# Sliding-window attention and spatial-shift MLP on one core: z tiles taken 13 products behind a block's transfer, the first four token tiles of QKV in two parts, Y's rows returned two blocks later, W1's casts moved

## The chip, the core and the metric

The kernel runs on one core of a Trainium2 chip. The metric is the device time of one execution in microseconds (us). Five engines run their own instruction streams in order: PE (TensorE), DVE (VectorE), ACT (ScalarE), POOL (GpSimd) and SP (SyncE, which here issues almost all DMAs). They meet only through semaphores, so an instruction that waits holds back all that stands behind it on its engine.

## What is computed

```python
x = A_x                                   # [1, 2048, 576], f32
xn = _layernorm(x)
return x + A(xn, wqkv, wo) + B(xn, w1, w2, w3, w4)
# A: qkv = xn @ wqkv, 32 heads of 18; each token attends to the 8 tokens
#    0, 2, ... 14 behind it; times wo
# B: z = _layernorm(xn); h = gelu(z @ w1); four quarters of h shifted by +1, -1, +2, -2 tokens;
#    x1 = xn + h_shifted @ w2; x1 + gelu(_layernorm(x1) @ w3) @ w4
```

## The kernel before

Tokens are 16 tiles of 128; `Y[:, t, :]` holds tile t's 576 columns. Products are made in pairs of rounded parts: a cast on ACT gives the high part, a subtraction on DVE the low part, and PE adds three of the four partial products. Three stages matter here.

**QKV, plain part (0 to 86 us).** `wqkv` is cut in six column groups `cg` of 288. `units` lists 36 pairs (t, cg), each 14 matmuls (`q_part`, L396) into a PSUM tile `p1`, then a copy to a staging tile and a spill to DRAM (`q_leave`, L401 and L384). The first tiles are written out by hand ahead of the loop. A token tile gets there by `stats_x` and `norm_x` (DVE, with a power on POOL between them, L113), `tails` (a POOL copy of 64 columns, widened, L295), `turn_x`/`turn_main` and `turn_tail` (PE transposes into the PSUM tile `ps`, L303 and L307), and `cast_main`/`cast_tail` (ACT high part, DVE low part). Then the dictionaries `mids` and `plan` say which side work follows which unit. A tensor's tile counts as one thing: what writes into a PSUM tile waits for the earlier reads of the same tile.

**QKV, Strassen part (86 to 216 us).** Tiles 6 to 15 are done in blocks p = 3..7 of two tiles, each three column groups `g` of seven products of seven matmuls (`step`, `seven`, L581). A block has 21 slots, one for each product; `plan[slot]` lists side work that is issued after it. During block p the operands of the next block, n = p + 1, are made: `prep_lower` (slot 3) and `prep_upper` (slot 7), both through the one PSUM tile `pp`, then casts. ACT's `act.copy(raw[:, 2, :], ...)` (L357) and DVE's L358 write to rows of Y that `away` has spilled to DRAM (`ysp`, L547) to make room. Beside this each block makes z for four token tiles, twice-normalized x: `z_turn` scales on ACT and transposes on DVE into the one tile `ST` (L129, L130), and `put` sends `ST` to DRAM (`xd`, L137, four DMAs). A z tile of the next block can be written to `ST` only when these DMAs have read it. In block 7 `get` fetches z's first 512 tokens back and `split_x` casts them; `split_w1` casts W1, which lies in Y's first five rows.

**Mixing (216 to 284 us).** For four blocks b of 512 tokens, `mix_tile` makes four tiles of h (L715) and `mix_rem` (L730) the rest with W1R, whose parts travel by `v<-u` DMAs. z of block b + 2 is fetched at the end of block b, and its casts stand on ACT between two gelus (L720, L721). `back` (L572) reads the eight spilled rows of Y again.

SP issues all these DMAs in program order. In all of it the order is that of the code.

Of the kernel before, what the change touches and what calls it, by code (L numbers as in the profile page):

```python
# [57 lines left out]
def fused_block(ctx, tc, x, wqkv, wo, w1, w2, w3, w4, out):  # L58
# [85 lines left out]

    def split_x(xt, part=None, scr=None):
        raw = xt.bitcast(F32)
        if part != 1:
            r = xt[:, 9, :] if scr is None else scr.bitcast(F32R)
            act.copy(r[64:128], raw[64:128, 4, :])
# [3 lines left out]
        for h in range(2) if part is None else (part,):  # L153
# [55 lines left out]
    def load_x(t):  # L209
        sp.dma_start(Y[:, t, :], xf[t * 128:(t + 1) * 128, :])  # L210

    counted, scaled = set(), {}

    def stats_x(t):
        stats(Y[:, t, :], 0, t)
        counted.add(t)

    def norm_x(t):
        norm(Y[:, t, :], Y[:, t, :], 0, t)
        lo = t - t % 2  # L220
        if not scaled.get(lo) and counted >= {lo, lo + 1}:
            scaled[lo] = True
            two = slice(lo, lo + 2)
# [4 lines left out]
            for k in (lo, lo + 1):  # L228
                pool.tensor_tensor(RS[1][:, k, 1:2], RS[1][:, k, 0:1], mhalf, op=ALU.pow)

    qraw = {}
# [18 lines left out]
    def flat(v):  # L250
        return v.rearrange("p o s c -> p o (s c)")
# [102 lines left out]
    def prep_lower(p, ps):  # L354
        turned(2 * p + 1, ps)
        raw = raw_s(p)
        act.copy(raw[:, 2, :], ps[:, 0, 0:384])  # L357
        dve.tensor_tensor(raw[:, 0, :], ps[:, 1, 0:384], raw[:, 2, :], op=ALU.add)  # L358
        cast_a(x_ops(("p", p)), 2, 1, ps[:, 1:2, :])

    def prep_upper(p, ps):
        turned(2 * p, ps)
# [72 lines left out]
    for i in range(24):  # L435
# [25 lines left out]
    cast_x(1, True)  # L461
    q_part(pq[1], 1, 0, 0, 12)
    norm_x(2)
    tails(2)
    q_part(pq[0], 0, 0, 12, 14)
    q_leave(pq[0], 0, 0)
    q_part(pq[1], 1, 0, 12, 14)
    stats_x(3)
    turn_x(2)
    turn_tail(2, turns[2])  # L470
    q_leave(pq[1], 1, 0)
    norm_x(3)
# [20 lines left out]
    mids = {2: lambda: prep_x(3), 19: lambda: prep_x(4),  # L493
            20: lambda: prep_x(5), 28: lambda: lower(3), 30: lambda: upper(3)}
    plan = {
            2: ((split_cg, 3),),
            3: ((load_x, 5), (lambda: load_cg(2, raw_tile("rawc")),)),
            4: ((sums_b, 0, 0),), 5: ((sums_b, 0, 1),),
            6: ((split_cg, 1),), 7: ((split_t, 0, False),),
            8: ((lambda: load_cg(5, raw_tile("rawb")),),),  # L500
# [4 lines left out]
            20: ((sums_b, 2, 0), (load_x, 9)), 21: ((sums_b, 2, 1),), 22: ((stats_x, 7),),  # L505
            23: ((norm_x, 7), (tails, 7)), 24: ((stats_x, 6),), 25: ((norm_x, 6), (tails, 6)),
            26: ((split_t, 0, True),), 27: ((split_t, 2, False),),
            28: ((split_t, 1, True), (load_x, 11)),
            30: ((lambda: cast_upper(3, two[3]),), (load_x, 10)), 31: ((cast_s, 3, 0),),
            32: ((cast_s, 3, 1), (stats_x, 9)), 33: ((cast_s, 3, 2),), 34: ((split_t, 2, True),),  # L510
            35: ((norm_x, 9), (stats_x, 8))}
    for n, (t, cg) in list(enumerate(units))[2:]:
        q_plain(t, cg, mids.get(n))
        for f, *args in plan.get(n, ()):
            f(*args)
# [124 lines left out]
    for p in range(3, 8):  # L640
        n = p + 1
        if n < 8:
            q4 = 4 * (p - 3)
            zs = (q4 + 1, q4 + 2, q4 + 3, q4) if p == 4 else range(q4, q4 + 4)
            plan = {k: ((z_turn, t),) for k, t in zip((1, 9, 10, 17), zs)}
            plan.update({0: ((norm_x, 2 * n),), 3: ((low2, n),), 4: ((tails, 2 * n),),
                         7: ((up2, n),), 8: ((lambda n=n: cast_upper(n, two[n]),),),
                         14: ((cast_s, n, 0),), 15: ((cast_s, n, 1), (cast_s, n, 2))})
            plan[17] += ((put, ("z", p - 3)),)
            if n < 7:  # L650
                plan[4] += ((stats_x, 2 * n + 3),)
                plan[16] = ((stats_x, 2 * n + 2),)
                plan[17] += ((norm_x, 2 * n + 3), (tails, 2 * n + 3))
            plan[18] = {3: ((load_x, 13), (load_x, 12), (away, 0, 3)),
                        4: ((load_x, 15), (load_x, 14), (away, 3, 5))}.get(p, ())
            if p == 4:
                plan[11] = ((away, 5, 8),)
            if p == 5:
                plan[11] = ((load_w1,),)
# [1062 lines left out]
```

## Time and profile before

| | us |
|---|---|
| three runs: median (lowest, highest) | 1310.93 (1308.13, 1311.07) |
| the profiled execution: its time | 1308.89 |
| its span from first to last instruction | 1307.1 |
| mean granted TensorE clock | 0.987 |

The page gives each engine's busy share of the span; the waits give, for each engine, who ended its idle time; a timeline gives single instructions with the idle time ahead of each in square brackets and what released them. Matmuls overlap their weight loads, so PE is near full where its share is 97 to 99%.

### The profile page before, as it was taken

The numbers are of one execution on the slowest core, as the hardware profiler recorded it, in microseconds if no ns is written. First come the engines' busy times: TensorE is split into PE (matmuls) and PEld (weight loads), VectorE is DVE, ScalarE is ACT, GpSimd is POOL, SyncE is SP. The second block draws the span as 40 slices with busy tenths as digits, with TensorE's granted clock in tenths as the row PEclk, the third lists the DMA queues.
The fourth block names the chain that finished last, engine by engine and source line by source line (L and its number), as shares of the span: only waits on it lengthen the run. The fifth ranks groups of instructions, "written<-read, shape, count | busy, mean of one in ns | idle before, by whom it ended". The sixth has DMA issues, their size and how long they took to land.

```text
span 1307.1 us, 21009 instructions
## 1 busy us (share of the span) xinstructions
PE 1268.6 (97%) x7819; PEld 1166.0 (89%) x7819; DVE 933.2 (71%) x1206; ACT 766.1 (59%) x1276; POOL 264.3 (20%) x407
## 2 busy tenths in 40 slices
PE   8997888999999999999999999999999999999999
PEld 7997887789889999999879999999989989889898
DVE  7875544476847898999657898898999884455342
ACT  4453445443654554554677767777667777677730
POOL 3121100002132212111212322222123223222100
PEclk9998889899999999999999999999999999999999
DMA  8535767525688879587948898887967878899982
GB/s 228 142 78 145 195 143 195 157 70 174 183 189 215 200 184 183 118 193 168 203 100 197 179 204 198 185 174 180 271 126 156 165 135 155 190 219 217 252 255 82
DMA packets 208654, 228.92 MB, mean 175 GB/s; under 512 B 80920, under 2 KB 142328, under 8 KB 208424
## 3 DMA queue, kind: packets, MB, share of 16 engines
q1 hardware_dynamic: 175800, 160.79, 43.0%
q0 software_dynamic: 32752, 66.80, 31.8%
q8 instruction: 61, 1.00, 0.3%
q14 instruction: 41, 0.34, 0.1%
HBM read 127.71 MB, written 110.23 MB: 182 GB/s over the span
## 4 chain that ended last, share of the span: by engine, by line
PE 63%; issue 3%; ACT 2%; DVE 2%; DMA 1%; POOL 0%; DVEq 0%; POOLq 0%; ACTq 0%
PE ps L1120 30%; PE cc L1382 19%; PE p L1084 10%; PE ps L183 4%; DMA yd<-Y 1%; DVE xt L849 0%; DVE w3st L1217 0%; POOL yd L1126 0%; ACT Y L1125 0%; PE p L1689 0%; ACT xt L1179 0%; ACT Y L1067 0%; DVE c L1078 0%; DVE Y L1131 0%; ACT c L1072 0%
## 5 line engine op out<-in xcount | busy, mean ns | idle before, releaser
L1120 PEld LDWEIGHTS ps<-w,c 128*128 128x128 f32 x3456 | 478.8, 189 | 21.1 <-ACT Y L1125 2.0
L1120 PE MATMUL ps<-w,c 128*128 128x288 f32 x3456 | 489.9, 297 | 5.1 <-DVE c L1078 1.4
L1126 POOL DMA_DIRECT2D yd<-Y x154 | 138.1, 900 | 395.8 <-ACT Y L1125 336.3
L1078 DVE TENSOR_TENSOR c<-Y,c 128x512 fp32r<-128x512 f32 x144 | 98.9, 687 | 93.2 <-ACT Y L1067 91.7
L1125 ACT COPY Y<-ps 128x576 f32<-128x576 f32 x154 | 97.9, 637 | 76.1 <-PE ps L1120 66.1
L1382 PE MATMUL cc<-xt,w3s 128*128 128x512 f32 (+1 forms) x504 | 127.9, 393 | 0.9 <-DVE Y L1392 0.9
L1382 PEld LDWEIGHTS cc<-xt,w3s 128*128 128x128 f32 (+1 forms) x504 | 92.2, 188 | 19.3 <-DVE Y L1392 1.3
L1128 ACT COPY Y<-ps 128x576 f32<-128x576 f32 x92 | 58.9, 640 | 66.2 <-PE ps L1120 64.5
L1382 PE MATMUL cc<-x1n,w3a 128*128 128x512 f32 (+1 forms) x336 | 86.4, 396 | 0.0
L998 DVE TENSOR_TENSOR po<-q,k 128x1152 f32<-128x1152 f32 (+1 forms) x48 | 84.2, 1755 | 0.8
L1001 DVE TENSOR_REDUCE L<-po 128x64 f32<-128x1152 f32 (+1 forms) x48 | 84.0, 1751 | 0.8
L1066 ACT ACTIVATE c<-p 128x512 fp32r<-128x512 f32 x48 | 28.7, 597 | 85.5 <-PE p L1084 85.5
L1392 DVE TENSOR_TENSOR Y<-cc,Y 128x512 f32<-128x512 f32 x49 | 33.7, 688 | 59.4 <-ACT Y L1388 55.2
L974 DVE TENSOR_TENSOR po<-v,L 128x1152 f32<-128x1152 f32 x56 | 75.4, 1354 | 0.9
L396 PE MATMUL p<-wb,xt 128*128 128x288 f32 (+1 forms) x504 | 71.2, 299 | 2.1 <-ACT stg L401 0.8
L396 PEld LDWEIGHTS p<-wb,xt 128*128 128x128 f32 (+1 forms) x504 | 67.7, 189 | 4.1 <-ACT stg L401 1.0
L1382 PEld LDWEIGHTS cc<-x1n,w3a 128*128 128x128 f32 (+1 forms) x336 | 61.3, 190 | 11.3 <-DVE w3a L1228 0.5
L113 POOL TENSOR_TENSOR rs<-rs,mhalf 128x1 f32<-128x1 f32 x32 | 19.5, 609 | 237.0 <-DVE rs L112 118.6
L978 DVE TENSOR_TENSOR po<-po 128x1152 f32<-128x1152 f32 x49 | 66.4, 1355 | 0.9
L581 PE MATMUL ca<-wb,xt 128*128 128x288 f32 x420 | 65.0, 307 | 1.8 <-DVE keep L592 1.3
L581 PEld LDWEIGHTS ca<-wb,xt 128*128 128x128 f32 x420 | 61.2, 200 | 2.7 <-DVE keep L592 1.8
L1101 ACT COPY ps<-Y 128x576 f32<-128x576 f32 x92 | 59.4, 646 | 4.4 <-DVE Y L1131 2.4
(255 smaller groups left out, 2158.2 us busy)
## 6 DMA issues: line engine op xcount, KB each, us to landing
yd<-Y POOLq DMA_DIRECT2D x156, 288.0 KB, 6.2
Y<-in_B_w_dram SPq DMA_DIRECT2D x29, 576.0 KB, 5.9
w3st<-in_B_w_dram SPq DMA_DIRECT2D x56, 256.0 KB, 8.1
qkvd<-stg SPq DMA_DIRECT2D x66, 144.0 KB, 3.0
yd<-ev POOLq DMA_DIRECT2D x26, 288.0 KB, 6.4
w3st<-in_B_w_dram SPq DMA_DIRECT2D x92, 64.0 KB, 8.0
xd<-st SPq DMA_DIRECT2D x16, 320.0 KB, 4.9
xd<-big SPq DMA_DIRECT2D x16, 320.0 KB, 6.4
```

Of the source, the lines that this page charges most:

```text
L396: pe.matmul(ps[:, :QB], xo[:n, o + k, a, :], W[:n, w + k, v, :], start=i == 0, stop=i == len(PLAIN) - 1)
L581: pe.matmul(ps[:, :QB], xo[:n, XO[x], a, :], W[:n, OP[w], v, :], start=start and i == 0, stop=stop and i == len(HALVES) - 1, skip_group_ch ...
L974: dve.tensor_tensor(dst, vv, Lf[:, :, w:w + 1].to_broadcast([128, TPP * GH, HD]), op=ALU.mult)
L978: dve.tensor_tensor(o, o, dst, op=ALU.add)
L998: dve.tensor_tensor(dst, qf[:, None, :].to_broadcast([128, n, TPP * GC]), win, op=ALU.mult)
L1001: dve.tensor_reduce(Lw[:, w:w + n, :], dst.rearrange("p w (x d) -> p w x d", d=HD), axis=AX.X, op=ALU.add)
L1078: dve.tensor_tensor(h[:, 1, :], g, h[:, 0, :].bitcast(F32), op=ALU.subtract)
L1084: pe.matmul(ps, W3[f][:, w, :], x1n[b][:, a, :], start=n == 0, stop=n == len(PAIRS) - 1)
L1120: pe.matmul(ps[:, k, :HF], h[:, col], w[:, p, k * HF:(k + 1) * HF], start=n == 0 and not seed, stop=n == len(seq) - 1, skip_group_check=True)
L1125: act.copy(e.rearrange("p (h c) -> p h c", h=2), ps[:, :, :HF])
L1126: pool.dma_start(yd[t], e, accum_op=ALU.add)
L1382: pe.matmul(ps, WX[w][:k, v, SLOT[w], :], area[sb][xk][:k, a, :], start=onto is None and i == 0, stop=last and i == len(HALVES) - 1, skip_ ...
```

## The change

- `split_x` takes parts: 0 (tail and first half, as before), 2 (tail alone), 3 (first half alone), 1 (second half).
- The powers for z (`scales`) are no longer issued in `norm_x` but at slots of the plans; the first weight group's tail is subtracted on POOL and not on DVE.
- The first four token tiles: tiles 2 and 3 too are done in two parts, with their casts ahead of the tail transposes; some loads change places.
- `prep_lower` casts first and adds then. In blocks 3 to 6 z tiles stand at slots 9, 10, 16, 17 (before: 1, 9, 10, 17), the two `stats_x` at slots 2 and 4 (before: 4 and 16).
- Block 7: z's fetch at slot 3 (before: 6), another order in its first group, z's casts at slots 12, 15 and 18, W1's first part at 14, the second and third behind the block, the last two in mixing after tiles 0 and 1.
- `back` is called at (b, i) = (2, 0) and not at (0, 3).

```diff
     def norm_x(t):
         norm(Y[:, t, :], Y[:, t, :], 0, t)
...
@@ prep_lower
         act.copy(raw[:, 2, :], ps[:, 0, 0:384])
+        cast_a(x_ops(("p", p)), 2, 1, ps[:, 1:2, :])
         dve.tensor_tensor(raw[:, 0, :], ps[:, 1, 0:384], raw[:, 2, :], op=ALU.add)
-        cast_a(x_ops(("p", p)), 2, 1, ps[:, 1:2, :])
@@ first tiles
-    split_tail(r0, 0, 0)
+    split_tail(r0, 0, 0, pool)
     cast_x(0, True)
+    cast_x(1, True)
+    q_head(1)
+    load_cg(1, raw_rows(10))
     stats_x(2)
...
     norm_x(2)
     tails(2)
...
+    q_tail(0)
+    turn_x(2)
     stats_x(3)
-    turn_x(2)
+    q_tail(1)
+    cast_x(2)
     turn_tail(2, turns[2])
-    q_leave(pq[1], 1, 0)
     norm_x(3)
     tails(3)
...
+    q_head(2)
+    cast_x(2, True)
+    turn_x(3)
+    cast_x(3)
+    q_tail(2)
+    turn_tail(3, turns[3])
+    cast_x(3, True)
+    split_cg(3)
+    q_head(3)
+    q_tail(3)
@@ blocks 3 to 6
-            plan = {k: ((z_turn, t),) for k, t in zip((1, 9, 10, 17), zs)}
+            plan = {k: ((z_turn, t),) for k, t in zip((9, 10, 16, 17), zs)}
...
             if n < 7:
-                plan[4] += ((stats_x, 2 * n + 3),)
-                plan[16] = ((stats_x, 2 * n + 2),)
+                plan[2] = ((stats_x, 2 * n + 3),)
+                plan[4] += ((stats_x, 2 * n + 2),)
@@ block 7
-            plan = {6: ((lambda: get(("z", 0), ring_block(("z", 0))),),),
-                    12: ((open_w1,), (split_w1, 0)), 14: ((split_w1, 1),),
-                    15: ((lambda: split_x(xring["z", 0], 0),),),
-                    17: ((lambda: split_x(xring["z", 0], 1),),)}
+            zx = xring
+            plan = {3: ((lambda: get(("z", 0), ring_block(("z", 0))),),),
+                    12: ((lambda: split_x(zx["z", 0], 2),),),
+                    14: ((open_w1,), (split_w1, 0)),
+                    15: ((lambda: split_x(zx["z", 0], 3),),),
+                    18: ((lambda: split_x(zx["z", 0], 1),),)}
...
+            if g == NGQ - 3:
+                order = ((g, 1), (g - 1, 4), (g - 1, 3), (g, 5), (g, 6), (g, 2), (g, 7))
...
+    split_w1(1)
+    split_w1(2)
     get(("z", 1), ring_block(("z", 1)))
@@ mixing
+            if b == 0 and i < 2:
+                split_w1(4 - i)
...
-            if b == 0 and i < 3:
-                split_w1((2, 4, 3)[i])
-            if (b, i) == (0, 3):
+            if (b, i) == (2, 0):
                 back()
```

In the built programs the change moves instructions as follows at three places. The line numbers of the changed kernel are a little other than those of before; where they differ, the sentence behind a pair gives both.

DVE at the start of block 5 (tiles 10 and 11 being multiplied, operands of block 6 being made), before: `st` is ST, `pp` the PSUM tile of `prep_lower`, `bn` the statistics of the next x tile (15).

```order
L120 TENSOR_SCALAR Y_71<-Y_71,mv0_77,rs0_80 128x576 [waits Pool_49]
L129 STREAM_TRANSPOSE st_1158<-z_1745 128x16x32 [waits DMAHW5_49,DMAHW6_49,DMAHW4_49,DMAHW7_49,DVE_49,Activation_49]
L130 STREAM_TRANSPOSE st_1158<-z_1745 128x4x32 [waits DVE_49]
L358 TENSOR_TENSOR Y_71<-pp_1768,Y_71 128x384 [waits Activation_49]
L326 TENSOR_TENSOR xt_1777<-pp_1768,xt_1777 128x256 [waits PE_49,Activation_49]
L328 TENSOR_TENSOR xt_1777<-pp_1768,xt_1777 32x128
L592 TENSOR_TENSOR keep_1673<-cc0_1637,keep_1673 128x288 [waits DMAHW3_49]
L110 BN_STATS bn_83<-Y_71 128x6 [waits DMAHW1_49]
```

The same place in the changed kernel:

```order
L120 TENSOR_SCALAR Y_71<-Y_71,mv0_77,rs0_80 128x576 [waits Pool_49]
L110 BN_STATS bn_83<-Y_71 128x6 [waits DMAHW1_49]
L110 BN_STATS bn_83<-Y_71 128x6
L111 BN_AGGR mv0_77<-bn_83 128x2 [waits DVE_49]
L112 TENSOR_SCALAR rs0_80<-mv0_77 128x1 [waits DVE_49]
L323 TENSOR_TENSOR xt_1772<-pp_1764,xt_1772 128x256 [waits PE_49,Activation_49]
L325 TENSOR_TENSOR xt_1772<-pp_1764,xt_1772 32x128
L356 TENSOR_TENSOR Y_71<-pp_1764,Y_71 128x384 [waits DMAHW6_49]
```

The transposes into ST are gone from this place, and tile 15's statistics, which stood behind the three reads of `pp` (L326, L328, L358, now L323, L325, L356), stand ahead of them; they wait for a DMA, the load of x tile 15.

PE in the head, from token tile 2's transposes on, before: `ps_284` and `ps_328` are the PSUM tiles of token tiles 2 and 3, `p1_320` the product of tile 2.

```order
L303 MATMUL ps_284<-ident_72,Y_71 128x128 [waits DVE_49]
L303 MATMUL ps_284<-ident_72,Y_71 128x128 x3
L307 MATMUL ps_284<-ident_72,stg_270 128x128 [waits Pool_49]
L307 MATMUL ps_284<-ident_72,stg_270 128x128
L396 MATMUL p1_320<-wb0_116,xt_221 128x288 [waits Activation_49]
L396 MATMUL p1_320<-wb0_116,xt_221 128x288 x6
L303 MATMUL ps_328<-ident_72,Y_71 128x128 [waits DVE_49,PE_49]
L303 MATMUL ps_328<-ident_72,Y_71 128x128 x3
L307 MATMUL ps_328<-ident_72,stg_300 128x128 [waits Pool_49]
```

The same in the changed kernel, where tiles 2 and 3 are `ps_278` and `ps_315`, and `p1_246` and `p1_300` the products of tiles 1 and 2:

```order
L300 MATMUL ps_278<-ident_72,Y_71 128x128 [waits DVE_49]
L300 MATMUL ps_278<-ident_72,Y_71 128x128 x3
L393 MATMUL p1_246<-wb0_116,xt_204 128x288 [waits Activation_49]
L393 MATMUL p1_246<-wb0_116,xt_204 128x288
L304 MATMUL ps_278<-ident_72,stg_271 128x128 [waits DVE_49,Pool_49]
L304 MATMUL ps_278<-ident_72,stg_271 128x128
L393 MATMUL p1_300<-wb0_116,xt_204 128x288 [waits Activation_49]
L393 MATMUL p1_300<-wb0_116,xt_204 128x288 x11
L300 MATMUL ps_315<-ident_72,Y_71 128x128 [waits DVE_49,PE_49]
L300 MATMUL ps_315<-ident_72,Y_71 128x128 x3
L393 MATMUL p1_300<-wb0_116,xt_204 128x288 [waits DVE_49]
L393 MATMUL p1_300<-wb0_116,xt_204 128x288
```

The tail transposes (L304, before L307) now wait for DVE as well as for POOL: DVE's cast of the main part, which reads the same PSUM tile, stands ahead of them (tile 3's, behind these rows, too). Tile 2's product runs to its twelfth matmul before tile 3 is transposed, not to its seventh.

SP behind the remainder of mixing block 0, before: `v` is the exchange of the remainder, `ysp` the spilled rows, `xt<-xd` the fetch of z for block 2.

```order
L736 DMA v_2634<-u_2633 16x512 [waits DMAHW5_49]
L572 DMA Y_71<-ysp0_1171 128x576 [waits DMAHW6_49,DVE_49]
L572 DMA Y_71<-ysp1_1172 128x576 [waits DMAHW7_49]
L572 DMA Y_71<-ysp2_1173 128x576 [waits DMAHW0_49]
L572 DMA Y_71<-ysp3_1174 128x576 [waits DMAHW1_49]
L572 DMA Y_71<-ysp4_1175 128x576 [waits DMAHW2_49]
L572 DMA Y_71<-ysp5_1176 128x576 [waits DMAHW3_49,Pool_49]
L572 DMA Y_71<-ysp6_1177 128x576 [waits DMAHW4_49,Pool_49]
L572 DMA Y_71<-ysp7_1178 128x576 [waits DMAHW5_49]
L142 DMA xt_2671<-xd_1963 128x3x512 [waits DMAHW6_49,PE_49]
L142 DMA xt_2671<-xd_1963 128x2x512 [waits DMAHW7_49]
```

The same in the changed kernel:

```order
L755 DMA v_2634<-u_2633 16x512 [waits DMAHW5_49]
L142 DMA xt_2663<-xd_1968 128x3x512 [waits DMAHW6_49,PE_49]
L142 DMA xt_2663<-xd_1968 128x2x512 [waits DMAHW7_49]
L720 DMA w2r_2668<-in_B_w2_dram 128x576 [waits DMAHW0_49,DVE_49]
L720 DMA w2r_2720<-in_B_w2_dram 128x576 [waits DMAHW1_49,DVE_49]
```

The eight loads of Y's rows stood between the exchange and z's fetch; they now come a block and a half later, behind the fetch of z for block 3.

More of the change, by code (lines that the diff above doesn't have):

```diff
@@ L146, in split_x @@
         raw = xt.bitcast(F32)
-        if part != 1:
+        if part in (None, 0, 2):
             r = xt[:, 9, :] if scr is None else scr.bitcast(F32R)
@@ L152, in split_x @@
                               op=ALU.subtract)
-        for h in range(2) if part is None else (part,):
+        for h in {None: (0, 1), 0: (0,), 1: (1,), 2: (), 3: (0,)}[part]:
             hi, lo = slice(2 * h, 2 * h + 2), slice(2 * h + 5, 2 * h + 7)
@@ L210, in load_x, with scales @@
         sp.dma_start(Y[:, t, :], xf[t * 128:(t + 1) * 128, :])
-    counted, scaled = set(), {}
     def stats_x(t):
         stats(Y[:, t, :], 0, t)
-        counted.add(t)
     def norm_x(t):
         norm(Y[:, t, :], Y[:, t, :], 0, t)
[L220 to L223, printed above, removed]
+    def scales(*ts):
+        for t in ts:
+            two = slice(t, t + 2)
             r = RS[1][:, two, 0:1]
@@ L227, in norm_x @@
             pool.tensor_tensor(r, r, eps, op=ALU.add)
-            for k in (lo, lo + 1):
+            for k in (t, t + 1):
                 pool.tensor_tensor(RS[1][:, k, 1:2], RS[1][:, k, 0:1], mhalf, op=ALU.pow)
@@ L443, in fused_block @@
     r0 = qraw[0]
+    x0 = plain_x(0)[0]
     hi_main(r0, 0, 0, 0)
@@ L504, in fused_block @@
             16: ((stats_x, 5),), 17: ((norm_x, 5), (load_x, 8), (tails, 5)), 18: ((split_cg, 5),),
-            20: ((sums_b, 2, 0), (load_x, 9)), 21: ((sums_b, 2, 1),), 22: ((stats_x, 7),),
+            20: ((sums_b, 2, 0), (load_x, 9)), 21: ((sums_b, 2, 1), (scales, 0, 2)),
+            22: ((stats_x, 7),),
             23: ((norm_x, 7), (tails, 7)), 24: ((stats_x, 6),), 25: ((norm_x, 6), (tails, 6)),
[L507 to L512, printed above, removed]
+            26: ((split_t, 0, True),), 27: ((split_t, 1, True), (load_x, 11)),
+            28: ((stats_x, 9),), 29: ((norm_x, 9), (load_x, 10)),
+            30: ((lambda: cast_upper(3, two[3]),),), 31: ((cast_s, 3, 0),),
+            32: ((cast_s, 3, 1),), 33: ((cast_s, 3, 2), (stats_x, 8)),
+            34: ((split_t, 2, False),), 35: ((split_t, 2, True),)}
+    for n, (t, cg) in list(enumerate(units))[4:]:
         q_plain(t, cg, mids.get(n))
@@ L650, in fused_block @@
             if n < 7:
-                plan[4] += ((stats_x, 2 * n + 3),)
-                plan[16] = ((stats_x, 2 * n + 2),)
+                plan[2] = ((stats_x, 2 * n + 3),)
+                plan[4] += ((stats_x, 2 * n + 2),)
                 plan[17] += ((norm_x, 2 * n + 3), (tails, 2 * n + 3))
+            plan[11] = {3: ((scales, 4, 6),), 4: ((away, 5, 8), (scales, 8, 10)),
+                        5: ((load_w1,), (scales, 12, 14)), 6: ()}[p]
             plan[18] = {3: ((load_x, 13), (load_x, 12), (away, 0, 3)),
                         4: ((load_x, 15), (load_x, 14), (away, 3, 5))}.get(p, ())
[L656 to L659, printed above, removed]
-        else:
-            plan = {6: ((lambda: get(("z", 0), ring_block(("z", 0))),),),
-                    12: ((open_w1,), (split_w1, 0)), 14: ((split_w1, 1),),
-                    15: ((lambda: split_x(xring["z", 0], 0),),),
-                    17: ((lambda: split_x(xring["z", 0], 1),),)}
+        else:
+            zx = xring
[4 more added lines that the diff above has]
+                    18: ((lambda: split_x(zx["z", 0], 1),),)}
         slot = 0
```

38 lines of the change are left out of this document (18 added, 20 removed).

## The prediction

> **What bounds the kernel now.** I read the page's busy shares first, then PE's waits, then the timelines around the longest of these. In the waits the columns are total us, times, longest.
>
> ```profile
> PE 1268.6 (97%) x7819; PEld 1166.0 (89%) x7819; DVE 933.2 (71%) x1206; ACT 766.1 (59%) x1276; POOL 264.3 (20%) x407
> ...
> PE pp L303 <- DVE xt L328: 14.7, 3, 7.6
> PE ps L715 <- ACT g L721: 2.9, 1, 2.9
> PE ps L730 <- DVE W1R L169: 1.7, 1, 1.7
> ...
> PE pp L307 <- POOL tl L295: 1.0, 1, 1.0
> ```
>
> PE is the bound, and the change takes no matmul away, so it can only win PE's idle time and what follows from it: 1307.1 - 1268.6 = 38.5 us idle, of which the first three of these waits are 19.3. All three lie in stages that the change touches. The first is the transpose at slot 7 (`prep_upper`) in blocks 4, 5 and 6:
>
> ```profile
> 122.23 1.09 PE L303 MATMUL pp<-ident,Y 128*128 128x128 f32 x4 [7.58 <-DVE xt L328]
> 149.24 1.09 PE L303 MATMUL pp<-ident,Y 128*128 128x128 f32 x4 [3.56 <-DVE xt L328]
> 176.42 1.08 PE L303 MATMUL pp<-ident,Y 128*128 128x128 f32 x4 [3.57 <-DVE xt L328]
> ```
>
> PE waits there for DVE to have read `pp`. What held DVE in blocks 5 and 6, and ACT in block 4, stands in their timelines:
>
> ```profile
> 119.63 0.48 ACT L357 COPY Y<-pp 128x384 f32<-128x384 f32 x1 [8.94 <-DMA ysp<-Y]
> ...
> 146.36 0.71 DVE L129 STREAM_TRANSPOSE st<-z 128x512 f32<-128x512 f32 x1 [7.34 <-DMA xd<-st]
> 147.19 0.52 DVE L358 TENSOR_TENSOR Y<-pp,Y 128x384 f32<-128x384 f32 x1
> 148.36 0.42 DVE L326 TENSOR_TENSOR xt<-pp,xt 128x256 fp32r<-128x256 f32 x1 [0.65 <-ACT xt L325]
> 148.80 0.29 DVE L328 TENSOR_TENSOR xt<-pp,xt 32x128 fp32r<-32x128 f32 x1
> 149.49 0.81 DVE L110 BATCH_NORM_STATS2 bn<-Y 128x6 f32<-128x288 f32 x2
> 150.58 0.15 DVE L112 TENSOR_SCALAR rs<-mv 128x1 f32<-128x1 f32 x1
> ...
> 173.55 0.71 DVE L129 STREAM_TRANSPOSE st<-z 128x512 f32<-128x512 f32 x1 [7.36 <-DMA xd<-st]
> ```
>
> So the three stalls are not one. In blocks 5 and 6 DVE's z transpose at slot 1 waits for `put` of the block before. In block 4 ACT waits until 119.63 for a spill of Y, and PE would wait with or without z. Each stall costs more than its wait, since the granted clock (third column below) falls and stays down:
>
> ```profile
> 147.00:148.00 1.00, 0.00 (x0) 0.94 0.87 214
> 148.00:149.00 1.00, 0.00 (x0) 0.50 1.03 399
> ...
> 154.00:155.00 1.00, 1.00 (x7) 0.65 0.11 21
> 155.00:156.00 1.00, 1.00 (x9) 1.00 0.50 121
> ...
> 250.00:251.00 1.00, 0.06 (x1) 0.64 0.00 0
> ...
> 257.00:258.00 1.00, 1.00 (x5) 0.95 0.28 62
> ```
>
> PE resumes at 149.24 and has half the clock until about 154.7: 5.4 us in which half the work is done, 2.7 us lost. Around 250 it is 250.94 to 257.1, 3.1 us lost.
>
> **The change part by part**
>
> *Block 6.* z's transposes go from slot 1 to slot 9. Here no x tiles are left to load, and nothing else waits ahead of the casts. The wait of 3.57 goes with the loss at half clock (2.8, between the two above): **-6.4**. Slot 9 has its own wait to meet:
>
> ```profile
> 164.54 4.14 SPq L137 DMA_DIRECT2D xd<-st  x4
> ...
> 207.40 1.09 PE L581 MATMUL cc<-wb,xt 128*128 128x288 f32 x7
> 208.33 1.10 PE L581 MATMUL ca<-wb,xt 128*128 128x288 f32 x7
> ```
>
> `put` was issued from 164.54 and its last read was over at 173.55, 9.0 us later. Products follow each other in 0.93 us, so 13 of them and the twelve transposes of `pp` take some 13 us: 4 us of room.
>
> *Block 5.* Here the old wait goes too, but x tile 15's statistics now stand ahead of DVE's reads of `pp`, and they wait for a load that SP issues behind `put`:
>
> ```profile
> 143.39 2.40 SPq L210 DMA_DIRECT2D Y<-in_A_x_dram  x2
> Y<-in_A_x_dram SPq DMA_DIRECT2D x1, 288.0 KB, 5.5
> ```
>
> The second row is the first of the two loads alone, tile 15: it lands 5.5 us after issue, at 148.9. SP's order up to it is unchanged. Statistics take 1.24 us (149.49 to 150.73 above), L326 and L328 0.44 + 0.29, L358 0.52: PE goes on at 148.9 + 2.6 = 151.5 and not at 149.24, **+2.3**. The loss at half clock stays. At best this load is as early as the casts need it, and block 5 wins 6.4 like block 6; at worst it lands 1 us later.
>
> *Block 4.* Tile 13's statistics wait too, but the spill that ACT waits for comes later than that load in SP's queue and still ends at 119.63. The new order of `prep_lower` lets L324 go without waiting for L358, which then comes last: 0.2 less. **-0.2**.
>
> *Block 3* begins with two weight casts that stood earlier (T3 and T1 of the third group). ACT's copy of the first product comes about 1 us later, but PE waited 1.0 us there for `tl` (the last of the waits above) anyway. I take 0, between -0.3 and +1.
>
> *Head.*
>
> ```profile
> 14.31 0.66 PE L303 MATMUL ps<-ident,Y 128*128 128x128 f32 x4 [0.26 <-DVE Y L120]
> 15.25 0.59 ACT L324 CAST xt<-ps 128x512 fp32r<-128x512 f32 x1 [0.76 <-PE ps L307]
> 16.70 0.69 DVE L326 TENSOR_TENSOR xt<-ps,xt 128x512 fp32r<-128x512 f32 x1
> 18.73 3.85 PE L396 MATMUL p<-wb,xt 128*128 128x288 f32 x27
> ```
>
> Before, PE runs without a gap from 18.73 and begins unit 4 after 21 more matmuls of 0.134 (3.85 less a tail of 0.25, for 27), at 21.5. After, tile 2's statistics stand behind one more tail cast, I estimate 0.4, so its transposes begin at 14.7 and end 0.66 later; ACT's cast comes behind a copy of tile 1's product, at 15.9 (0.6), DVE's at 16.55 (0.69), and only at its end, 17.25, PE may make the tail transposes, then 12 matmuls (1.6), to 19.1. Tile 3's transposes take 0.66 and its two casts 0.6 and 0.7, so its tail transposes start at 21.15, and 14 matmuls later unit 4 begins at 23.25. **+1.7**, between 0 (if the casts hide behind products after all) and +2.5. The powers that leave POOL and the tail cast that goes there lie beside this and free nothing PE waits for.
>
> *Block 7.*
>
> ```profile
> 202.29 1.07 SPq L142 DMA_DIRECT2D xt<-xd  x2
> xt<-xd SPq DMA_DIRECT2D x1, 768.0 KB, 5.4
> 206.37 1.20 PE L581 MATMUL ca<-wb,xt 128*128 128x288 f32 x7 [0.48 <-DVE keep L592]
> ```
>
> The fetch is asked for three products earlier, but SP is behind with `put` and spills, so it moves up by two spills only, to about 200.8, and lands at 206.2. PE is due at slot 15 at 205.9 (206.37 - 0.48), so z's tail cast, behind slot 12, stands ready three products sooner, at some 204, and waits 2 us for the data. ACT's cast (0.62, its row below), DVE's and DVE's sum behind them take 1.8, I estimate, and PE, which needs the sum, goes on at 208.0. That is 2.1 in place of 0.48; the two later waits (0.52 and 0.82 before) become about 0.3. **+0.1**, from -1.5 to +3.
>
> *Mixing.* W1R's cast moves from behind tile 1 to behind tile 0, 14 matmuls earlier, which is more than its wait: **-1.7**. The third wait:
>
> ```profile
> 235.62 3.84 SPq L572 DMA_DIRECT2D Y<-ysp  x8
> 239.56 1.20 SPq L142 DMA_DIRECT2D xt<-xd  x2
> xt<-xd SPq DMA_DIRECT2D x1, 768.0 KB, 7.6
> 247.14 0.62 ACT L149 CAST xt<-xt 64x512 fp32r<-64x512 f32 x1 [5.90 <-DMA xt<-xd]
> 250.94 12.69 PE L715 MATMUL ps<-xt,W 128*128 128x512 f32 x42 [2.90 <-ACT g L721]
> ```
>
> ACT waits 5.9 us for z of block 2, the gelus behind it free their PSUM tiles late, and PE waits 2.9. That fetch was issued behind eight loads of Y (3.84 us) and took 7.6 us with their data ahead of it, where one without takes 5.4. Without them it lands 3.84 + 2.2 = 6.0 us sooner, which is all of ACT's wait. So 2.9 + 3.1 go: **-6.0**. The eight loads now come behind z of block 3, and the residual sums read Y only after the last mixing block. If they delayed the exchange `v<-u` behind them, ACT would wait in block 3, with three PSUM tiles of slack; I take 0, and up to +3.
>
> Everything after 284 us only moves along, as PE is the chain there. **Sum**: -6.4 + 2.3 - 0.2 + 0 + 1.7 + 0.1 - 1.7 - 6.0 = -10.2, from the profiled execution's 1308.89 to 1298.7. That execution lay 2.0 below the median of the runs shown, 1310.93, and from there the sum gives 1300.7; I predict 1300.
>
> **The clock at the new short waits.** In the rows above PE falls idle at 145.7 (149.24 - 3.56) and 248.0 (250.94 - 2.90), and the clock, by the means of its first slow slices, at 147.9 and 250.3: 2.2 us of idling were enough. Block 7's new wait is 2.1, the head's new ones come out at 1.3 to 2.0. So by the rows block 7's stands on the edge, and it is a rival below.
>
> The Trainium skill, "TensorE: Matmul & The Clock Gate", "Part 1: The HAM clock gate", says that the clock halves after at least one idle window of some 3.4 us on a free-running count. By that rule no new wait is long enough and the sum stays 1300. The trace disagrees with that length: 2.2 here.
>
> **The rivals**
> - *Block 5 wins too*, because the load of tile 15 is early enough. For it: its time rests on one row. Against it: PE was due at 145.7 and the casts take 2.6, so 5.8 us would have to be found, and SP's order up to the load is the same. 1300 - 2.3 - 6.4 = 1291. Chance 0.12.
> - *The clock drops in block 7*, the wait being a little longer than I make it: +2.8, 1303. Chance 0.25.
> - *z of block 2 is late still*, as SP still issues the eight DMAs of the exchange ahead of it: 1306. Chance 0.08.
> - *Most of it comes to nothing*: head and block 3 at their bad ends, block 7's clock down: +0.8 + 1 + 2.8 and the exchange late by 3, 1308. Chance 0.07.
> - *The wait for `put` only moves*, to slot 9 of blocks 4, 5 and 6, now ahead of DVE's sums that free PE's accumulators. It decides from a `put` of over 13 us; the traced one took 9.0. At 18 us PE would wait about 5 in each block and lose 2.8 of clock: 3 x 7.8 = 23 more, 1323, slower. For it speaks only that DVE is already a term of PE's waits there; no `put` in the rows takes that long. Chance 0.04.
>
> **How the numbers follow.** The forecast has the remaining 0.44. A measurement of this kernel can tell about 0.3%, 4 us, from no change, so faster means below 1307: the forecast, the first two rivals and most of the third, 0.84, less something for a stall that I don't see, 0.82; within 0.3%: 0.13; slower: 0.05. The range leaves out the last rival and the tail of the fourth: 1289 to 1308, the first rival with its error below, the fourth above.
>
> **What would show it.** Block 6: no wait of PE at slot 7, clock 1.0 throughout. Block 5: DVE's L110 idle until a load of x, PE's transposes 5 to 6 us late; block 4: ACT's copy still released by `ysp`. Head: PE's tail transposes released by DVE, unit 4 at 23. Block 7: DVE's sum late by z's fetch. Mixing: PE without waits. I am wrong if block 5 has no stall, if the clock drops somewhere new, or if ACT still waits for z of block 2.

## The result and the profile after

The changed kernel takes 1301.55 us (median of 4 runs, 1301.08 to 1302.03), the kernel before on the same chip 1310.47 (4 runs): a ratio of 0.9935, 95% interval 0.9918 to 0.9952. The forecast was 1300. The profiled execution took 1301.31 with a span of 1299.5, which is 7.6 less than before.

First the page's share of PE and PE's waits (total us, times, longest), in the changed kernel:

```profile
PE 1265.0 (97%) x7819; PEld 1166.5 (90%) x7819; DVE 932.0 (72%) x1205; ACT 765.2 (59%) x1276; POOL 264.5 (20%) x408
...
PE pp L300 <- DVE Y L356: 12.4, 2, 7.5
PE ps L304 <- DVE xt L312: 3.0, 2, 1.8
PE ca L596 <- DVE keep L607: 2.9, 2, 2.6
PE ps L300 <- DVE Y L120: 2.1, 2, 1.7
PE ps L1139 <- ACT ev L1144: 2.0, 1, 2.0
```

Of the three stalls at `pp` two are left; the mixing's two waits (gelus, W1R) are gone from the list; new are the head's (L304), block 7's (`ca`) and one at L1139, the first down products, a stage that the change does not touch (`x1n` below is normalized x1, fetched back from DRAM; `ev` is the tile to which ACT copies finished sums out of PSUM). The timeline of the changed kernel says who held each:

```profile
17.44 0.66 PE L304 MATMUL ps<-ident,stg 128*128 128x128 f32 x2 [1.79 <-DVE xt L312]
...
22.69 0.41 PE L304 MATMUL ps<-ident,stg 128*128 128x128 f32 x2 [1.23 <-DVE xt L312]
...
121.29 0.48 ACT L354 COPY Y<-pp 128x384 f32<-128x384 f32 x1 [9.09 <-DMA ysp<-Y]
...
123.70 1.09 PE L300 MATMUL pp<-ident,Y 128*128 128x128 f32 x4 [7.54 <-DVE Y L356]
...
149.56 0.82 DVE L110 BATCH_NORM_STATS2 bn<-Y 128x6 f32<-128x288 f32 x2 [8.87 <-DMA Y<-in_A_x_dram]
...
152.31 1.09 PE L300 MATMUL pp<-ident,Y 128*128 128x128 f32 x4 [4.86 <-DVE Y L356]
...
175.33 0.60 PE L300 MATMUL pp<-ident,Y 128*128 128x128 f32 x4
...
202.97 0.61 ACT L149 CAST xt<-xt 64x512 fp32r<-64x512 f32 x1 [2.16 <-DMA xt<-xd]
...
204.85 2.05 PE L596 MATMUL ca<-wb,xt 128*128 128x288 f32 x7 [2.62 <-DVE keep L607]
...
341.61 0.38 SPq L863 DMA_DIRECT2D x1n<-xn  x1
...
349.55 0.63 ACT L877 ACTIVATE Y<-x1n 64x512 fp32r<-64x512 f32 x1 [2.57 <-DMA x1n<-xn]
...
353.31 2.02 PE L1139 MATMUL ps<-w,c 128*128 128x288 f32 x12 [1.97 <-ACT ev L1144]
```

Block 4 (121 to 124) stalls on the spill as before, block 5 (149 to 152) on x tile 15's load, block 6 (175) not at all; block 7 (203 to 205) waits for z's fetch through ACT and DVE. In the head PE's two waits (17 and 23) are for DVE's casts, and behind the first of them the granted clock, the third number from the end in these windows, is halved; in the kernel before it was 1.00 from 5 to 30 us:

```profile
17.00:18.00 1.00, 0.56 (x3) 0.59 (x4) 0.78 (x2) 0.00 (x0) 0.09 (x1) 0.50 0.60 148
...
20.00:21.00 1.00, 1.00 (x10) 1.00 (x8) 0.00 (x0) 0.00 (x0) 0.00 (x0) 0.82 0.00 0
```

Reading the start of each stage off PE's two timelines (`mm_tok` makes the products behind mixing) gives the change of each stage's length, from one execution of each kernel:

| stage | start before | start after | forecast of its change | measured |
|---|---|---|---|---|
| up to block 3 (head) | 0 | 0 | +1.7 | +1.95 |
| block 3 | 85.79 | 87.74 | 0 | -0.4 |
| block 4 | 106.34 | 107.87 | -0.2 | +0.25 |
| block 5 | 137.38 | 139.16 | +2.3 | +0.9 |
| block 6 | 164.52 | 167.21 | -6.4 | -6.3 |
| block 7 | 191.75 | 188.10 | +0.1 | +2.25 |
| mixing | 215.79 | 214.39 | -7.7 | -9.0 |
| from `mm_tok` on | 283.80 | 273.40 | 0 | +2.8 |
| whole span | 1307.1 | 1299.5 | -10.2 | -7.6 |

So the size came out as forecast within a few us, partly because errors of both signs met: less lost in block 5 and more won in mixing, but 2.15 more lost in block 7, and 2.8 given back in a stage in which I expected nothing. The head's agreement is a sum of two such errors too, as the account below says.

### The profile page after: what moved, and what is told of

Its sections match the earlier page's. It is cut to its first block, busy times and chain, and to the rows that moved or that the text cites. A ratio compares the mean times of both kernels' runs of the same rounds, so it can differ in the third digit from the quotient of the medians.

```text
span 1299.5 us, 21014 instructions
## 1 busy us (share of the span) xinstructions
PE 1265.0 (97%) x7819; PEld 1166.5 (90%) x7819; DVE 932.0 (72%) x1205; ACT 765.2 (59%) x1276; POOL 264.5 (20%) x408
## 4 chain that ended last, share of the span: by engine, by line
PE 64%; DVE 2%; ACT 2%; DMA 1%; issue 1%; SPq 0%; DVEq 0%; ACTq 0%
PE ps L1139 31%; PE cc L1401 19%; PE p L1103 9%; PE ps L183 4%; DMA td0T<-xn 1%; DVE po L1017 1%; DMA xt<-xn 1%; DVE xt L868 0%; DVE w3st L1236 0%; DVE c L1097 0%; PE p L1708 0%; ACT Y L1144 0%; ACT xt L1198 0%; DVE L L1020 0%; DVE Y L1150 0%
## 5 line engine op out<-in xcount | busy, mean ns | idle before, releaser
L1139 PEld LDWEIGHTS ps<-w,c 128*128 128x128 f32 x3456 | 478.7, 189 | 22.3 <-ACT ev L1144 2.2
L1139 PE MATMUL ps<-w,c 128*128 128x288 f32 x3456 | 489.7, 297 | 6.6 <-ACT ev L1144 2.0
```

The lines of the kernel that those rows point to most:

```text
L1139: pe.matmul(ps[:, k, :HF], h[:, col], w[:, p, k * HF:(k + 1) * HF], start=n == 0 and not seed, stop=n == len(seq) - 1, skip_group_check=True)
```

## The experiments

Each is the changed kernel with the edit shown, timed in rounds beside the kernel before. Ratios are to the latter. Each trace is one execution and can lie away from its median: those of e6 (1296.06) and e11 (1278.48) are the lowest of their runs, that of e3 (1302.63) the highest. The intervals of e2, e3, e5, e6 and e10 overlap that of the changed kernel's first runs; there the traces decide, not the medians.

| run | median us (runs) | lowest to highest | ratio, 95% interval |
|---|---|---|---|
| e1 z's slots back | 1306.28 (12) | 1301.46 to 1308.06 | 0.9968, 0.9955 to 0.9980 |
| e2 statistics back | 1300.98 (6) | 1299.24 to 1305.27 | 0.9941, 0.9923 to 0.9960 |
| e3 spill earlier | 1298.06 (6) | 1296.42 to 1302.63 | 0.9916, 0.9899 to 0.9933 |
| e4 Y back early | 1308.11 (12) | 1305.53 to 1312.14 | 0.9990, 0.9977 to 1.0003 |
| e5 block 7 | 1297.66 (6) | 1294.63 to 1302.32 | 0.9911, 0.9892 to 0.9930 |
| e6 head | 1302.21 (6) | 1296.06 to 1304.62 | 0.9934, 0.9914 to 0.9954 |
| e7 loads earlier | 1292.43 (4) | 1288.87 to 1295.14 | 0.9860, 0.9842 to 0.9878 |
| e9 loads and spill | 1286.29 (4) | 1284.91 to 1287.31 | 0.9817, 0.9804 to 0.9830 |
| e8 = e9 + e5 + e6 | 1282.72 (4) | 1281.36 to 1284.12 | 0.9790, 0.9777 to 0.9804 |
| e10 W3's pair later | 1302.16 (5) | 1300.26 to 1303.13 | 0.9934, 0.9921 to 0.9947 |
| e11 = e8 + e10 + a spill | 1281.16 (5) | 1278.48 to 1282.79 | 0.9779, 0.9766 to 0.9792 |
| e12 unchanged, again | 1303.09 (6) | 1300.45 to 1305.23 | 0.9942, 0.9927 to 0.9957 |

**e1: z's transposes at their old slots.**

```diff
-            plan = {k: ((z_turn, t),) for k, t in zip((9, 10, 16, 17), zs)}
+            plan = {k: ((z_turn, t),) for k, t in zip((1, 9, 10, 17), zs)}
```

> Only the slots of z's transposes are undone (1, 9, 10, 17 in blocks 4 to 6). Theory (block 6's gain is the wait of z's transpose for put, taken off DVE's way): block 6 gets its stall at slot 7 back, about 3.6 us of wait and 2.8 at half clock, and block 5 stays as it is, since tile 15's load holds DVE anyway: 1301.5 + 6.4 = 1308. Rival (block 6 gained through what else left that stage, the statistics at slot 16 or W1's load): 1301.5, no stall in block 6.

The timeline of e1 in block 6, and then its clock (windows: us, PE busy, ..., granted clock as the third number from the end):

```profile
177.84 0.71 DVE L129 STREAM_TRANSPOSE st<-z 128x512 f32<-128x512 f32 x1 [7.80 <-DMA xd<-st]
...
180.09 0.63 PE L300 MATMUL pp<-ident,Y 128*128 128x128 f32 x4 [2.90 <-DVE Y L356]
```

```profile
174.90:178.30 3.40, 2.29 (x18) 2.05 (x16) 0.46 (x1) 0.85 (x3) 0.00 (x0) 1.00 1.04 201
178.30:181.70 3.40, 1.60 (x13) 1.64 (x14) 3.06 (x9) 0.00 (x0) 0.00 (x0) 1.00 0.55 101
```

The stall is back, with the releaser of the kernel before: `put`. So block 6's gain is the place of z's transposes. But only the wait of 2.9 came back, the clock stayed at 1.00: block 6 is 3.1 us longer than in the changed kernel (24.0 and 20.9). The edit moves block 3's z tiles too, which the expectation left out, and block 3 is 1.1 longer. The median is 4.7 us above the first four runs of the changed kernel and 3.2 above e12, not 6.4. How the clock can stay is shown by e12.

**e2: only the statistics of tile 2n + 3 behind the casts again.**

```diff
-                plan[2] = ((stats_x, 2 * n + 3),)
-                plan[4] += ((stats_x, 2 * n + 2),)
+                plan[4] += ((stats_x, 2 * n + 3), (stats_x, 2 * n + 2))
```

> Only the statistics of x tile 2n+3 go back from slot 2 to slot 4, behind the casts that read pp. Theory (tile 15's load, landing at about 149.5, is the cause, and the place of the statistics only says which product meets it): PE's wait at slot 7 of block 5 (4.86) goes, DVE's sum behind the statistics is late instead and PE waits some 2.4 at slot 9; 1301.5 - 2.4 = 1299, and the clock still drops or does not, up to 1.6 more. Rival (DVE has slack there): no wait in block 5, 1301.5 - 4.9 - 2 = 1294.5. Block 4 stays in both, since ACT waits there for ysp.

The timeline of e2 in block 5:

```profile
151.77 0.82 DVE L110 BATCH_NORM_STATS2 bn<-Y 128x6 f32<-128x288 f32 x2 [3.68 <-DMA Y<-in_A_x_dram]
...
154.62 3.48 PE L596 MATMUL ca<-wb,xt 128*128 128x288 f32 x14 [4.42 <-DVE keep L607]
```

The wait at `pp` is gone and stands two products later, at the accumulator that DVE's sum frees, 4.42 in place of 4.86 (I had 2.4; the load came at 151.77 here, not at 149.5, and two sets of statistics stand ahead of the sum). The time does not differ from the changed kernel's. So it isn't the place of the statistics on DVE that costs block 5 its gain, as the prediction's wording suggests, but the late load.

**e3, e7 and e9: the two transfers.** e3 asks for the spill earlier, e7 for the loads, e9 for both.

```diff
 e3, e9
-            plan[11] = {3: ((scales, 4, 6),), ...
+            plan[11] = {3: ((scales, 4, 6), (away, 0, 3)), ...
 e7, e9
+            plan[16] += {3: ((load_x, 13), (load_x, 12)),
+                         4: ((load_x, 15), (load_x, 14))}.get(p, ())
 e3: slot 18 of block 3 keeps the loads; e7: it keeps the spill; e9: neither
```

> Only the spill of rows 0 to 2 of Y is asked for at slot 11 of block 3 and not at slot 18 behind the loads. Theory (block 4's stall is this spill, and tile 13's load is next behind it): ACT's wait of 9.1 in block 4 goes, DVE's statistics wait for the load until about 118, PE goes on at 120.5 and not at 123.7: 1301.5 - 3.2 = 1298. Rival (the spill waits for bandwidth and not for its place): no change, 1301.5.

> Only the loads of x tiles 12 to 15 move, from slot 18 to slot 16, ahead of put; the spill of rows 0 to 2 stays at slot 18. Theory (block 5's stall is tile 15's load alone, block 4's the spill alone as long as it comes last): no wait at slot 7 of block 5, which is 4.9 + 1.6 shorter, while block 4 still waits 7 us on ACT and ysp: 1301.5 - 6.5 = 1295. Rival (both stalls come from the two transfers' sharing of bandwidth with put): both halve, 1293.

> The spill of rows 0 to 2 is asked for at slot 11 of block 3, and the loads of x tiles 12 to 15 at slot 16, ahead of put at slot 17, in place of slot 18. Theory (blocks 4 and 5 stall on these two transfers alone, which stand behind put): no wait of PE at slot 7 of blocks 4 and 5, clock 1.0 there; block 4 shorter by 7.5 + 2.7, block 5 by 4.9 + 1.6: 1301.5 - 16.7 = 1285. Rival (put, now behind two loads, comes late for z's transposes at slot 9, or the loads only swap places with put in the same bandwidth): a wait of 2 to 5 at slot 9 of blocks 4 to 6 and half the gain, 1293.

The timeline of e3 in block 4:

```profile
119.92 0.82 DVE L110 BATCH_NORM_STATS2 bn<-Y 128x6 f32<-128x288 f32 x2 [9.88 <-DMA Y<-in_A_x_dram]
...
122.56 1.09 PE L300 MATMUL pp<-ident,Y 128*128 128x128 f32 x4 [5.75 <-DVE Y L356]
```

That of e7 in blocks 4 and 5:

```profile
120.25 0.48 ACT L354 COPY Y<-pp 128x384 f32<-128x384 f32 x1 [6.95 <-DMA ysp<-Y]
...
122.66 1.09 PE L300 MATMUL pp<-ident,Y 128*128 128x128 f32 x4 [5.40 <-DVE Y L356]
...
139.60 0.82 DVE L110 BATCH_NORM_STATS2 bn<-Y 128x6 f32<-128x288 f32 x2 [1.22 <-DMA Y<-in_A_x_dram]
```

And the new group among PE's waits in e9, which has none at `pp`:

```profile
PE ca L596 <- ACT keep L629: 1.6, 2, 1.2
```

In e3 ACT no longer waits in block 4, and tile 13's load is next behind the spill, as forecast, but it landed at 119.9 and not at 118, so PE's wait fell from 7.54 to 5.75 only. In e7 block 5 has no wait and block 4 still has the spill's, 5.40 and not 7.54; the median, 1292.43, is nearer to the rival's number, but the waits aren't both halved: one is gone. With both, neither block waits. 1301.55 or 1303.09 to 1286.29: 15.3 to 16.8 for the expected 16.7. What remains of the rival is small: 1.6 us of waits for ACT, whose copies find `keep` not yet spilled.

**e4: only Y's return at its old place.**

```diff
-            if (b, i) == (2, 0):
+            if (b, i) == (0, 3):
                 back()
```

> Only the return of Y's rows goes back to mixing block 0, ahead of the fetch of z's block 2. Theory (the eight loads delay that fetch): ACT waits again about 6 us for z of block 2, PE 2.9 and then half clock for 3.1: mixing 6 longer, 1307.5. Rival (the stage gained through W1R's cast and the order of W1): mixing stays at 59.0, 1301.5.

The timeline of e4 in mixing:

```profile
246.00 0.62 ACT L149 CAST xt<-xt 64x512 fp32r<-64x512 f32 x1 [6.43 <-DMA xt<-xd]
...
249.81 2.11 PE L734 MATMUL ps<-xt,W 128*128 128x512 f32 x8 [3.43 <-ACT g L740]
```

ACT's wait for z of block 2 and PE's behind it are back (2.90 on PE in the kernel before), and the kernel costs 6.6 us more, or 5.0 against e12. The mixing stage takes 65.4 us here, 59.0 in the changed kernel: PE waits 5.45 in it in three places, and no half clock followed, where I expected 3.1 lost to it. The eight loads ahead of the fetch are the cause.

**e5: block 7's tail cast and W1's first cast exchanged.**

```diff
-                    12: ((lambda: split_x(zx["z", 0], 2),),),
-                    14: ((open_w1,), (split_w1, 0)),
+                    12: ((open_w1,), (split_w1, 0)),
+                    14: ((lambda: split_x(zx["z", 0], 2),),),
```

> Only two entries of block 7 change places: W1's pool and first cast at slot 12, z's tail cast at slot 14. Theory (the tail cast stands at ACT and DVE before its data is there, and DVE's sum behind it holds PE at slot 15): the wait of 2.62 and the short time at half clock after it go, block 7 is 2.5 to 3.5 shorter, 1298.5. Rival (the casts are late wherever they stand, or W1's cast at slot 12 waits for W0's last readers): the wait stays above 1.5 or moves to slot 13, 1301.5.

The timeline of e5:

```profile
202.29 1.20 PE L596 MATMUL ca<-wb,xt 128*128 128x288 f32 x7 [0.48 <-DVE keep L607]
...
203.15 0.62 ACT L149 CAST xt<-xt 64x512 fp32r<-64x512 f32 x1 [0.86 <-DMA xt<-xd]
```

The fetch lands no sooner (203.15, 202.97 above), but nothing that PE needs at slot 15 stands behind it: 0.48 in place of 2.62. The median is 3.9 below the first runs of the changed kernel, 5.4 below e12.

**e6: the head's tail transposes ahead of the main casts.**

```diff
     q_tail(1)
-    cast_x(2)
     turn_tail(2, turns[2])
+    cast_x(2)
+    cast_x(2, True)
     norm_x(3)
...
     q_head(2)
-    cast_x(2, True)
     turn_x(3)
-    cast_x(3)
     q_tail(2)
     turn_tail(3, turns[3])
+    cast_x(3)
     cast_x(3, True)
```

> Only tiles 2 and 3 of the head change: their tail transposes stand ahead of the casts of their main part again. Theory (in the changed kernel PE's tail transposes wait for DVE's cast, as both are in one PSUM tile): the waits of 1.79 and 1.23 go, block 3 begins 1.5 to 1.9 sooner, 1299.7. Rival (then PE waits for POOL's copies of the tails instead, 1.0 in the kernel before): 0.5 sooner at most, 1301.

PE's timeline in e6:

```profile
17.16 1.84 PE L393 MATMUL p<-wb,xt 128*128 128x288 f32 x12 [0.76 <-ACT xt L311]
19.45 0.63 PE L300 MATMUL ps<-ident,Y 128*128 128x128 f32 x4 [0.44 <-DVE Y L120]
...
21.38 32.09 PE L393 MATMUL p<-wb,xt 128*128 128x288 f32 x231 [0.81 <-ACT xt L311]
```

The two waits of 1.79 and 1.23 go, and three of 2.0 in all take their place, two of them for ACT's casts. Block 3 begins one us sooner (86.72, 87.74 above), but the clock stayed at 1.00 in this head, while half clock cost the changed kernel's head 1.5 us, so even that us isn't shown to be the edit's. The time shows no difference: nearer to the rival in size, but PE doesn't wait for POOL, which was the rival's reason. In e8 and e11, with the same edit, the head has half clock again (from 16.4 and 17.3, 3.4 us each).

**e8: e9, e5 and e6 together.**

> All three together: transfers earlier in blocks 3 and 4, block 7's two entries exchanged, the head's tail transposes ahead. Theory (the stalls are independent, as PE is the chain between them): the sum, 1301.5 - 16.7 - 3 - 1.8 = 1280. Rival (time won early is given back later, as 2.4 us were between 340 and 365 us, where PE waits for a fetch): 1284 to 1290.

1282.72, between the two. The first down products still wait 2.1 us there.

**e10: that last wait.** The timeline of the kernel before, at the fetch of `x1n`:

```profile
352.60 0.38 SPq L844 DMA_DIRECT2D x1n<-xn  x1
...
359.13 0.63 ACT L858 ACTIVATE Y<-x1n 64x512 fp32r<-64x512 f32 x1 [0.95 <-DMA x1n<-xn]
```

There it took 6.5 us, in the changed kernel 7.9 (341.61 to 349.55 above). ACT waits for it, and its copy to `ev`, which PE needs, stands behind.

```diff
                 get_n(2, x1n[2])
-                load_w3p(1, (0,))
...
             if (u, i) == (0, 1):
                 get_n(3, x1n[3])
+                load_w3p(1, (0,))
```

> Behind the QKV stage: W3's second pair (320 KB) is asked for behind the fetch of x1n's block 3 and not 1.6 us behind that of block 2. Theory (this load shares the DMA engines with the fetch that ACT waits for): the fetch takes 6.7 us and not 7.9, PE's wait of 2.0 at the first down products (L1139 on ev) is under 0.8 and no half clock follows: 1301.5 - 1.2 to 2.9 = 1299.5. Rival (the next put of xn, issued 5.2 us behind the fetch, is what slows its end): the wait stays near 2, 1301.5.

In e10 it takes 7.9 again (341.98 to 349.91 in its timeline) and PE waits 2.48: the theory falls. W3's load alone isn't the cause.

**e12: the changed kernel again**, to see what belongs to the program and what to the execution.

> The changed kernel itself again. Theory (the granted clock changes only on a grid of 3.41 us that runs free of the program; a window of it in which PE idles over about 1.9 us is followed by half clock, and one with under 1.0 ends it): the waits of blocks 4, 5 and 7 and of the first down products are the same within 0.6, the grid lies elsewhere, each stretch of half clock lasts 3.4, 6.8 or 10.2 us, and whether one follows the waits of 2.0 to 2.6 is another than in the first profile or the same by chance; times spread over 1295 to 1304. Rival (some 2.2 us of idling lower the clock, wherever they fall): half clock at the same places, and a spread of 1 us.

The granted clock around block 7's wait, by windows of the length of a stretch: first the changed kernel's first profile, then e12, then e10, which up to there is the same program.

```profile
201.20:204.60 3.40, 1.03 (x8) 0.80 (x7) 0.95 (x2) 1.61 (x4) 0.00 (x0) 1.00 1.02 313
204.60:208.00 3.40, 3.15 (x13) 3.15 (x14) 1.02 (x2) 1.65 (x3) 0.00 (x0) 0.51 1.15 180
208.00:211.40 3.40, 3.40 (x27) 3.40 (x26) 2.30 (x3) 2.03 (x4) 0.14 (x2) 0.99 0.18 43
...
351.40:354.80 3.40, 1.49 (x11) 1.49 (x12) 2.99 (x4) 3.40 (x7) 0.00 (x0) 1.00 0.62 159
354.80:358.20 3.40, 3.40 (x11) 2.75 (x11) 0.77 (x2) 0.77 (x2) 0.00 (x0) 0.51 0.57 176
```

```profile
203.00:206.40 3.40, 0.61 (x5) 0.45 (x4) 1.24 (x3) 2.18 (x4) 0.00 (x0) 0.99 1.12 290
206.40:209.80 3.40, 3.40 (x16) 3.40 (x15) 1.43 (x2) 1.73 (x3) 0.00 (x0) 0.51 1.11 187
...
353.10:356.50 3.40, 1.99 (x14) 1.95 (x15) 3.40 (x5) 3.11 (x7) 0.00 (x0) 1.00 0.47 116
356.50:359.90 3.40, 3.40 (x17) 2.79 (x16) 0.27 (x1) 0.84 (x2) 0.00 (x0) 1.00 0.76 267
```

```profile
201.50:204.90 3.40, 1.95 (x15) 1.72 (x13) 0.00 (x0) 0.58 (x2) 0.00 (x0) 1.00 1.02 294
204.90:208.30 3.40, 1.71 (x13) 1.71 (x14) 1.97 (x3) 2.47 (x6) 0.00 (x0) 1.00 1.31 254
```

PE waits 2.62, 2.79 and 3.14 us at this place. The longest of the three is the one without half clock: the grid cuts it into 1.45 and 1.69, and neither window is idle for long enough. At 353 the wait is 1.97 in the first profile and 1.98 in e12, and the clock halves in the first only. So the theory holds in what matters here: a wait's length alone does not decide. Three of its sizes were off. PE's wait in block 5 is 5.94 and not 4.86, since the load of tile 15 took 5.5 us from issue to landing and not 4.5; a window at half clock with 0.95 us of idling (from 151.7) did not end the stretch; and the times run up to 1305.23. In this execution block 5 takes 29.70 us, block 7 26.54 and the part from `mm_tok` on 1023.64, which against the kernel before is +2.6, +2.5 and +0.3.

**e11: everything that helped, W3's pair later, and the spill of rows 3 and 4 away from `put`.**

```diff
 e8 and e10, and
-            plan[18] = {4: ((away, 3, 5),)}.get(p, ())
+            plan[6] = {4: ((away, 3, 5),)}.get(p, ())
```

> All of the earlier edits together, W3's pair later as well, and the spill of rows 3 and 4 at slot 6 of block 4, away from put. Theory (stalls independent; the waits of 1.4 and 0.65 for ACT's keep in blocks 5 and 6 come from spills that stand in SP's queue behind put and that spill): 1282.7 - 2 - 1.2 = 1279.5. Rival (put alone holds the spills back, and the fetch stays slow): 1282.5.

The clock in e11, and its wait at the first down products:

```profile
120.00:160.00 40.00, 40.00 (x306) 40.00 (x306) 26.88 (x62) 21.84 (x52) 7.26 (x20) 1.00 0.95 233
160.00:200.00 40.00, 38.91 (x271) 37.21 (x270) 18.14 (x34) 22.19 (x45) 0.75 (x18) 1.00 0.84 182
```

```profile
332.06 1.86 PE L1140 MATMUL ps<-w,c 128*128 128x288 f32 x12 [0.80 <-ACT ev L1145]
```

1281.16, 2.2% below the kernel before and 1.6% below the changed one, though not to be told from e8. PE doesn't idle at all from 120 to 160 us. The fetch of `x1n` took 6.6 us here (321.66 to 328.29).

## Why the prediction was right, and where it was not

- **Block 6** (-6.4, measured -6.3): shown, by e1. The half clock in this sum is one that the kernel before had in its profiled execution; e1 has the same stall without it.
- **Block 5** (+2.3, measured +0.9): the mechanism was right, tile 15's load behind `put` (e2, e7). Mis-sized was the load's time: it landed 4.5 us after its issue (145.06 to 149.56) where I had 5.5, so the wait grew by 1.3 and not 2.3; and "the loss at half clock stays" was off too, 2.2 lost (152.31 to 156.8) and not 2.7. In e12 the load took 5.5, and block 5 is 2.6 longer than before. The place of the statistics decides only which product waits.
- **Block 4** (-0.2, measured +0.25): the spill holds ACT until 121.29 as said, and e3 and e9 show it is the cause.
- **Block 3** (0, measured -0.4): a little better than the range of -0.3 to +1.
- **Head** (+1.7, measured +1.95): the waits of 1.79 and 1.23 on DVE's casts are those forecast, but that the sum agrees is luck. Half clock from 16.9 to 20.4, with 2.9 us of work in it, cost 1.5 that the sum put at nothing, and unit 4 began at 24.8 and not 23.25 (21.6 before). Then 1.2 came back before block 3, of which 0.8 is a wait at 73.84 that only the kernel before has. What undoing the order of the casts brings isn't told from nothing (e6).
- **Block 7** (+0.1, measured +2.25): z's fetch holds ACT, DVE and then PE as forecast, but the wait was mis-sized, 2.62 and not 2.1, as the data came 0.4 us later in the block than I had it, and the rival's drop of the clock came with it: 3.15 us of work at half clock, 1.6 lost. e5 shows the order of the two casts to be the cause.
- **Mixing** (-7.7, measured -9.0): e4 shows Y's return to be worth 5.0 to 6.6, for 6.0 forecast. W1R's wait of 1.7 is gone too; for that part alone there was no run. The 1.3 beyond lie in no wait that the trace lists, but in PE's busy time, 1.2 less in this stage; why is open.
- **"Everything after 284 us only moves along"** is the step that failed: 2.8 us were given back in the first profile, nearly all of it between 340 and 365 us. A PE wait of 1.10 there shrank to 0.30, one of 0.34 grew to 1.97, and half clock from 354.8 to 358.2 took 1.7 more: +2.5. The half clock belongs to that execution: in e12 the wait is 1.98, none follows (nor at 670, where the kernel before has 3.4 us of it), and the stage is 0.3 longer than before. What both share is PE's idling in it, 11.8 and 12.2 us, 10.4 before. ACT waited 2.57 us for the fetch of `x1n`, 0.95 before. That fetch took 6.5 us before and 6.6 in e11, but 7.8 to 8.1 in the twelve other profiles; why is open. e10 rules out W3's load as the only cause.
- **"2.2 us of idling were enough"** failed as a rule: see the last section. By my own signs of being wrong one came true, "the clock drops somewhere new": it did in the head, in block 7 and at 354.8.
- **The total.** The time, 1301.55 and 1303.09 in e12, lies between the forecast (1300) and the rival with a drop in block 7 (1303), and that drop came. So the parts won are those forecast, for the reasons given, while the agreement to 2 or 3 us owes something to luck: the drops in the head and behind 340 us, which the sum lacks, were met by less lost in block 5 and more won in mixing.

## What to carry to other kernels

When a wait is moved off an engine, look for the transfer behind the one that it waited for: blocks 4 and 5 kept their stalls because a load and a spill stood behind the same `put`, and asking for them earlier won 15 us, more than the change itself. Put casts of fetched data behind the work that PE needs soon, not where the data might just be there. And don't price a stall by one profile: half clock behind it may be there in one execution of the same program and missing in the next.

## What the runs showed of the hardware

In windows of 0.2 us between 100 and 380 us, the granted clock was halved in 36 stretches over the 14 profiles of this case. All lasted 3.4, 6.8 or 10.2 us within 0.2, and within one profile all changes lie on one grid of 3.41 us: in the changed kernel at 119.4, 129.6, 150.0, 156.8, 204.6, 208.0, 354.8 and 358.2, where 354.8 - 119.4 is 69 times 3.41. The grid's phase differs from execution to execution. At full clock, and in that part of the span, no window of the grid in which PE idled 1.85 us or less was followed by half clock and every one with 1.90 or more was; at 1.87 (the first profile, from 351.4) it was, at 1.88 (e1, from 178.2) it wasn't. Outside that part the border lies lower and isn't sharp: a window with 1.65 was followed by half clock (e1, from 662.9), and of two with 1.70 in the head one was (e4, from 12.4) and one wasn't (e12, from 11.8). So idle time alone is not the whole rule. Of the windows at half clock, those with up to 0.5 us of idling were the last of their stretch, those with 0.7 or more were followed by another, and between these it went both ways. So a wait of 2 to 3.1 us costs itself alone, or itself and up to 1.7 us for each 3.4 us of half clock, by where it falls. In e5 this goes with the spread of the runs: the lowest, 1294.63, had a mean granted clock of 0.994 and the highest, 1302.32, one of 0.988, and 0.006 of some 1300 us is 7.8 us, for a spread of 7.7.

The Trainium skill, "TensorE: Matmul & The Clock Gate", "Part 1: The HAM clock gate", says that the clock follows an activity window of about 3.4 us that runs free of the program, and that it halves after an idle window. The stretches agree with the length and with running free; the windows quoted above disagree with "idle", since 1.49 us of work in 3.40 (351.40 to 354.80) did not keep the clock up.
